# Turning the second layer's weights to float32 early, beside the first layer's steady blocks

## The chip, the cores and the metric

The kernel runs on one core of a Trainium2 chip. The metric is the device time of one execution in microseconds (us); of several runs the median counts. Five engines work side by side, each through its own instructions in order: PE multiplies matrices, DVE, ACT and POOL work on elements, and SP does nothing here but issue DMAs, that is, transfers between DRAM and the on-chip memory.

## The reference

Three stages follow each other. Between them the data stay in float32; the weight arrays `w_gate`, `w_val`, `w_out` of the first layer and `w_in`, `w_out` of the second come as float64.

```python
# attention in both directions, 8 batches of 8 heads; x: 512 rows, state: 32 rows
a  = softmax(scale * x @ state.T);   xread = a @ state
a2 = softmax(scale * state @ x.T);   sread = a2 @ x
x = concatenate([xread, sread])              # 8 * 544 = 4352 rows of 512
# first layer, d_ff = 1536
x = (silu(x @ w_gate) * (x @ w_val)) @ w_out
# second layer, d_ff = 2048
h = x @ w2_in
out = (h * sigmoid(1.702 * h)) @ w2_out      # 4352 x 512
```

## The kernel before

**Numbers in pieces.** Each float32 operand of a matmul is cut into a high part that TensorE takes whole and a low part that holds the rest, and a product is three matmuls: high by high, high by low, low by high. So a piece of weights ends as a tile `wu` with two halves. The loader of the weights is one ordered list, `stream`. Each entry is a unit of 128 by 512 weights (`("o", i, f)` for the first layer's output weights, `("i2", f)` and `("o2", f)` for the second layer's), with its source, its place, and a DRAM tile to keep it in, if any. Three functions walk along the list. `w_dma` issues loads into `raw`, of which there are four buffers; they are shared with `ev`, through which finished rows leave. `w_begin` does the conversion where the source is float64: two ACT operations (lines 192 and 193), two DVE operations (194 and 195) and an addition on POOL (198) make the float32 tile `wt`, of which there are three. Where the source is float32, `w_begin` issues nothing and only marks the raw buffer as held. `w_end` makes the halves: an ACT copy (208) and a POOL subtraction (209), and it stores the float32 tile where there is one to keep (211). `need(key)` brings the list forward to a unit: it ends units one after the other and keeps two more begun. Loads run at most four raw buffers ahead, held ones included, and two in the last two steps of a block (`pos["ahead"]`).

**First layer.** It runs in nine blocks, here called block 0 to 8 in order of time; blocks 0 to 6 and block 8 hold 512 rows of one batch, block 7 holds the 256 rows that belong to the states (`tail` in the code). A block has twelve steps `f`. A step makes a product for the gate and one for the value into two alternating `gv` buffers, applies the sigmoid (`sg`), multiplies, cuts the result into the halves of `h`, and adds the output product of the step before into `acc` (`out1`). In between, by the tables START, BLOCK0 and GROUP, stand the pieces of the attention of the next batch, and `state_weights`, which multiplies the states into the gate and value weights of the steps to come. These pieces put their products in `at`, of which there are two buffers, and PE takes such a buffer again only when ACT and DVE have emptied it. At the end of a block ACT and DVE copy `acc` into two `ev` tiles and SP stores them (`y`).

**Weights of the first layer.** Block 0 converts `w_out` once and keeps it in DRAM as float32 (`w1o`); blocks 1 to 8 load it from there, one unit per step.

**Weights of the second layer.** All 32 units are loaded as float64 and converted where they are used: four in block 7 (`NEW`), 24 in block 8, the last four in the first steps of the second layer. In the list an odd step of block 7 and each step of block 8 has its units behind the unit `("o", i, f)`.

The order on each engine is the order in which this Python code issues the instructions; no scheduler moves them.

Of the kernel before, what the change touches and what calls it, by code (L numbers as in the profile page):

```python
# [8 lines left out]
F32 = mybir.dt.float32  # L9
# [70 lines left out]
def kernel(  # L80
# [26 lines left out]
    DM = H * D  # L107
    FF1 = w_gate.shape[1]
    FF2 = w2_in.shape[1]
    P = 128  # L110
# [3 lines left out]
    F2 = FF2 // P  # L114
# [6 lines left out]
    v, a, pe, pool_e, sy = nc.vector, nc.scalar, nc.tensor, nc.gpsimd, nc.sync  # L121
# [6 lines left out]
    dp = ctx.enter_context(tc.tile_pool(name="scratch", bufs=1, space=DRAM))  # L128
# [12 lines left out]
    def f32(t):  # L141
        return t.bitcast(F32)


    def src_in(w, f):
        return w[:, f * P : (f + 1) * P].rearrange("(k p) m -> p k m", p=P)

    def src_out(w, f):
        return w[f * P : (f + 1) * P, :].unsqueeze(1)

    stream = []
# [5 lines left out]
    pos = {"dma": 0, "begun": 0, "done": 0, "ahead": 4}  # L157
    RAWS = 4

    def add(key, src, loc, keep=None):  # L160
        where[key] = len(stream)
        stream.append((key, src, loc, keep))
# [39 lines left out]
        pos["begun"] += 1  # L202

    def w_end():
        key, src, (pl, tag, bufs), keep = stream[pos["done"]]
        t = temps.pop(key)
        u = (pl or x2p).tile([P, 2, DM], F32R, name="wu", tag=tag, bufs=bufs)
        a.copy(u[:, 0, :], t)  # L208
        pool_e.tensor_tensor(u[:, 1, :], t, f32(u[:, 0, :]), op=ALU.subtract)  # L209
        if keep is not None:  # L210
            sy.dma_start(keep, t)
        held.discard(key)
        units[key] = u
        pos["done"] += 1

    def w_step(lead=2):
        if pos["begun"] > pos["done"]:
            w_end()
        w_dma()
        while pos["begun"] < min(pos["done"] + lead, len(stream)):  # L220
            w_begin()
            w_dma()
# [307 lines left out]
    def add_gv(u, k):  # L530
        r, c = slice(k * P, (k + 1) * P), slice(u * 2 * P, (u + 1) * 2 * P)
        add(("gv", u, k), (w_gate[r, c], w_val[r, c]), (wp, f"w{u * KD + k}", 1))
# [3 lines left out]
    for f in range(F1):  # L536
        if f < F1 - 2:
            for k in range(2):
                add_gv(f // 2 + 1, f % 2 * 2 + k)
        add(("o", 0, f), src_out(w_out, f), (wp, "o", 2), w1o[f])  # L540
    for i in range(1, NB1 - 2):
        for f in range(F1):
            add(("o", i, f), w1o[f], (wp, "o", 2))

    units2 = []
    for f in range(F2):
        units2.append((("i2", f), src_in(w2_in, f)))
        units2.append((("o2", f), src_out(w2_out, f)))
    NEW = 4
    x2p = None  # L550

# [34 lines left out]
    def h_tile(n):  # L586
# [14 lines left out]
        "attn_state": lambda: attn_state(0),  # L601
        "begin": w_begin,
        "end": w_end,
        "sw0": lambda: state_weights(0, 0, 0),
        "sw1": lambda: state_weights(0, 0, 1),
# [39 lines left out]
    for i, blk in enumerate(order1):  # L645
# [39 lines left out]
        def w_beside(ops):  # L685

            for op in ops if i == 0 else "":
                if op == "E":
                    if pos["begun"] > pos["done"] and pos["done"] < where["o", 1, 0]:
                        w_end()  # L690
                    continue
                w_dma()
                if pos["begun"] < min(pos["done"] + 2, len(stream)) and stream[pos["begun"]][0] in raws:
                    w_begin()
                    w_dma()
# [148 lines left out]
```

## Time and profile before

| | us |
|---|---|
| median of three runs | 1674.04 (1673.78 to 1674.15) |
| the profiled execution, its own time | 1674.44 |
| its span, first to last instruction | 1672.7 |
| block 0, with the start | about 200 |
| blocks 1 to 5, each | 90.2 |
| block 6 | 91.4 |
| block 7 (256 rows) | 61.0 |
| block 8 | 108.5 |
| second layer | about 760 |

PE is busy for 1568 us, 94% of the span, DVE for 51%, ACT for 41%, POOL for 21%. The shares differ by stage. In the profile's picture of 40 slices PE stands at nine tenths or more from the fifth slice on, except for slices 19 to 22, which are blocks 7 and 8; there POOL goes up from two tenths to as much as eight and DVE up to eight. The granted clock of TensorE is at one of two levels, 1.2 or 2.4 GHz; a row gives its mean over a stretch as a share of the higher one. A block's end is read from its `y` stores on SP. The time of one execution is the span and 1.7 us around it.

### The profile page before, as it was taken

The numbers are of one execution on the slowest core, as the hardware profiler recorded it, in microseconds if no ns is written. First come the engines' busy times: TensorE is split into PE (matmuls) and PEld (weight loads), VectorE is DVE, ScalarE is ACT, GpSimd is POOL, SyncE is SP. The second block draws the span as 40 slices with busy tenths as digits, with TensorE's granted clock in tenths as the row PEclk, the third lists the DMA queues.
The fourth block names the chain that finished last, engine by engine and source line by source line (L and its number), as shares of the span: only waits on it lengthen the run. The fifth ranks groups of instructions, "written<-read, shape, count | busy, mean of one in ns | idle before, by whom it ended". The sixth has DMA issues, their size and how long they took to land.

```text
span 1672.7 us, 18772 instructions
## 1 busy us (share of the span) xinstructions
PE 1568.0 (94%) x7100; PEld 1274.6 (76%) x7100; DVE 859.8 (51%) x1361; ACT 682.1 (41%) x1217; POOL 350.7 (21%) x263
## 2 busy tenths in 40 slices
PE   4667899999999999989987999999999999999997
PEld 2445688888888888869765888888888888888886
DVE  5788766676767666654787333232322322222222
ACT  5566554545555454544565232222222222222222
POOL 3566322222222221225686020000000000000000
PEclk7788899999999999999999999999999999999999
DMA  4445321212122212223445001010101010000000
GB/s 144 126 137 151 103 52 48 77 42 82 49 67 59 64 45 80 52 76 108 145 157 176 19 0 45 7 45 7 41 10 38 13 38 13 32 20 29 10 26 14
DMA packets 85747, 102.40 MB, mean 61 GB/s; under 512 B 44184, under 2 KB 53400, under 8 KB 85656
## 3 DMA queue, kind: packets, MB, share of 16 engines
q1 hardware_dynamic: 85656, 101.21, 20.1%
q8 instruction: 55, 0.90, 0.2%
q14 instruction: 36, 0.29, 0.1%
HBM read 79.69 MB, written 21.50 MB: 60 GB/s over the span
## 4 chain that ended last, share of the span: by engine, by line
PE 45%; DVE 4%; ACT 1%; issue 1%; DMA 0%; DVEq 0%
PE gv L236 8%; PE gv L235 8%; PE gv L234 8%; PE acc L247 7%; PE acc L246 7%; PE acc L248 7%; DVE wt L195 2%; DVE wt L194 1%; ACT wu L208 0%; ACT wt L192 0%; ACT h L736 0%; DVE sg L730 0%; DVE sg L720 0%; DVE xl L571 0%; DMA raw<-in_moe_w_in_dram 0%
## 5 line engine op out<-in xcount | busy, mean ns | idle before, releaser
L805 DVE TENSOR_TENSOR sg<-gv,sg 128x512 f32<-128x512 f32 (+1 forms) x144 | 95.3, 662 | 426.1 <-ACT sg L804 426.1
L804 ACT ACTIVATE sg<-gv 128x512 f32<-128x512 f32 (+1 forms) x144 | 82.6, 574 | 442.1 <-PE gv L236 442.1
L236 PE MATMUL gv<-xl,wu 128*128 128x512 f32 (+1 forms) x576 | 219.5, 381 | 0.0
L235 PE MATMUL gv<-xh,wu 128*128 128x512 f32 (+1 forms) x576 | 219.2, 381 | 0.0
L234 PE MATMUL gv<-xh,wu 128*128 128x512 f32 (+1 forms) x576 | 219.0, 380 | 0.0
L209 POOL TENSOR_TENSOR wu<-raw,wu 128x512 fp32r<-128x512 f32 x96 | 126.0, 1312 | 425.3 <-ACT wu L208 392.9
L247 PE MATMUL acc<-wu,h 128*128 128x512 f32 x544 | 213.2, 392 | 0.0
L246 PE MATMUL acc<-wu,h 128*128 128x512 f32 x544 | 212.9, 391 | 0.0
L248 PE MATMUL acc<-wu,h 128*128 128x512 f32 x544 | 212.1, 390 | 0.0
L241 PE MATMUL gv<-a,xh 128*128 128x512 f32 x384 | 160.6, 418 | 14.9 <-DVE sg L730 10.0
L242 PE MATMUL gv<-a,xl 128*128 128x512 f32 x384 | 157.6, 410 | 16.8 <-DVE xl L571 16.8
L679 PE MATMUL acc<-h,wu 128*128 128x512 f32 (+1 forms) x432 | 167.0, 387 | 4.8 <-ACT h L736 4.8
L680 PE MATMUL acc<-h,wu 128*128 128x512 f32 (+1 forms) x432 | 165.5, 383 | 0.9 <-POOL wu L209 0.9
L681 PE MATMUL acc<-h,wu 128*128 128x512 f32 (+1 forms) x432 | 165.2, 382 | 1.0 <-DVE h L738 0.9
L243 PE MATMUL gv<-a,xh 128*128 128x512 f32 x384 | 156.3, 407 | 0.0
L571 DVE TENSOR_TENSOR h<-sg,h 128x512 fp32r<-128x512 f32 (+1 forms) x144 | 96.4, 670 | 95.4 <-ACT h L570 90.0
L570 ACT CAST h<-sg 128x512 fp32r<-128x512 f32 (+1 forms) x144 | 86.0, 597 | 105.6 <-DVE sg L805 105.6
L234 PEld LDWEIGHTS gv<-xh,wu 128*128 128x128 f32 x576 | 108.5, 188 | 22.3
L235 PEld LDWEIGHTS gv<-xh,wu 128*128 128x128 f32 x576 | 108.2, 188 | 22.2
L236 PEld LDWEIGHTS gv<-xl,wu 128*128 128x128 f32 x576 | 108.3, 188 | 21.8
L720 DVE TENSOR_TENSOR sg<-gv,sg 128x512 f32<-128x512 f32 (+1 forms) x108 | 71.2, 659 | 95.5 <-ACT sg L718 95.1
L246 PEld LDWEIGHTS acc<-wu,h 128*128 128x128 f32 x544 | 102.1, 188 | 22.5
(105 smaller groups left out, 2728.0 us busy)
## 6 DMA issues: line engine op xcount, KB each, us to landing
raw<-w1o SPq DMA_DIRECT2D x96, 256.0 KB
raw<-in_moe_w_out_dram SPq DMA_DIRECT2D x28, 512.0 KB
y<-ev SPq DMA_DIRECT2D x16, 512.0 KB
raw<-in_moe_w_in_dram SPq DMA_DIRECT2D x16, 512.0 KB
xr<-y SPq DMA_DIRECT2D x32, 256.0 KB
out_dram<-ev SPq DMA_DIRECT2D x16, 512.0 KB
xn<-in_x_dram SPq DMA_DIRECT2D x14, 512.0 KB
raw<-in_moe_w_gate_dram SPq DMA_DIRECT2D x24, 256.0 KB
```

Of the source, the lines that this page charges most:

```text
L234: pe.matmul(ps[:, :N], wh, xh, start=k == 0, stop=False)
L235: pe.matmul(ps[:, :N], wl, xh, start=False, stop=False)
L236: pe.matmul(ps[:, :N], wh, xl, start=False, stop=k == KD - 1)
L241: pe.matmul(ps, wh, xh, start=k == 0, stop=False)
L242: pe.matmul(ps, wl, xh, start=False, stop=False)
L243: pe.matmul(ps, wh, xl, start=False, stop=k == len(pairs) - 1)
L246: pe.matmul(ps, lh, rh, start=first, stop=False)
L247: pe.matmul(ps, lh, rl, start=False, stop=False)
L248: pe.matmul(ps, ll, rh, start=False, stop=last)
L679: pe.matmul(ps, w[:, 0, c], h[:, 0, :N], start=f == 0, stop=False)
L680: pe.matmul(ps, w[:, 1, c], h[:, 0, :N], start=False, stop=False)
L681: pe.matmul(ps, w[:, 0, c], h[:, 1, :N], start=False, stop=f == F1 - 1)
```

## The change

32 new entries go into the list: a second layer's unit stands behind each odd step's `("o", i, f)` of blocks 1 to 5 and behind those of steps 1 and 3 in block 6. Such an entry has a place of `None`. It is loaded as float64 and converted by `w_begin` like any other; `w_end` then only stores its `wt` in a DRAM tile of float32 (`w2i`, `w2o`). The entries of blocks 7 and 8 and of the second layer have these DRAM tiles as their source, so that they are loaded as float32 and `w_begin` issues nothing for them. All 32 units are moved; nothing else is computed differently.

```diff
     def w_end():
-        key, src, (pl, tag, bufs), keep = stream[pos["done"]]
+        key, src, loc, keep = stream[pos["done"]]
         t = temps.pop(key)
+        if loc is None:
+            sy.dma_start(keep, t)
+            pos["done"] += 1
+            return
+        pl, tag, bufs = loc
         u = (pl or x2p).tile([P, 2, DM], F32R, name="wu", tag=tag, bufs=bufs)
...
+    sources = []
+    for f in range(F2):
+        sources.append((("i2", f), src_in(w2_in, f)))
+        sources.append((("o2", f), src_out(w2_out, f)))
+    units2 = [(key, dp.tile([P, DM], F32, name=f"w2{key[0]}{key[1]}")) for key, _ in sources]
+    turns = iter(zip(sources, units2))
     for i in range(1, NB1 - 2):
         for f in range(F1):
             add(("o", i, f), w1o[f], (wp, "o", 2))
-
-    units2 = []
-    for f in range(F2):
-        units2.append((("i2", f), src_in(w2_in, f)))
-        units2.append((("o2", f), src_out(w2_out, f)))
+            turn = next(turns, None) if f % 2 else None
+            if turn:
+                add(("turn", turn[0][0]), turn[0][1], None, turn[1][1])
```

Lines behind the first edit stand 5 higher in the changed kernel, lines behind the second 10 higher: line 208 is 213, 331 is 336, 571 is 581, 730 is 740.

SP at the end of block 2 and the start of block 3, before: two stores of `y`, then loads of the first layer's output weights.

```order
L759 DMA y_2_0_3082<-ev 128x1024
L759 DMA y_2_2_3087<-ev 128x1024
L174 DMA raw<-w1o_103 128x512
L174 DMA raw<-w1o_104 128x512
L174 DMA raw<-w1o_105 128x512
```

The same place now (line 208 is the new store):

```order
L769 DMA y_2_0_3221<-ev 128x1024
L769 DMA y_2_2_3226<-ev 128x1024
L208 DMA w2o_124<-wt 128x512
L177 DMA raw<-in_moe_w_in_dram 128x4x128
L174 DMA raw<-w1o_103 128x512
L174 DMA raw<-w1o_104 128x512
L177 DMA raw<-in_moe_w_out_dram 128x512
```

A store and a float64 load have moved in ahead of the first float32 load, and behind the stores of `y`; the float64 load waits until the first of these two stores has been read out, since it takes its buffer.

DVE in the first step of block 3, before (`stz`: the states; `xtl`: low part of the turned input of the attention; `xl`: low part from `state_weights`):

```order
L720 TENSOR_TENSOR sg<-gv,sg 128x512
L294 TENSOR_TENSOR stz_95<-at,stz_95 128x4x64
L730 TENSOR_TENSOR sg<-gv,sg 128x512
L335 TENSOR_TENSOR xtl_3134<-at,xth_3133 128x512
L571 TENSOR_TENSOR xl<-at,xh 128x512
L738 TENSOR_TENSOR h<-sg,h 128x512
```

And now:

```order
L730 TENSOR_TENSOR sg<-gv,sg 128x512
L299 TENSOR_TENSOR stz_95<-at,stz_95 128x4x64
L194 TENSOR_SCALAR wt<-wt 128x512
L195 SCALAR_TENSOR_TENSOR wt<-raw,wt 128x512
L740 TENSOR_TENSOR sg<-gv,sg 128x512
L340 TENSOR_TENSOR xtl_3282<-at,xth_3281 128x512
L581 TENSOR_TENSOR xl<-at,xh 128x512
L748 TENSOR_TENSOR h<-sg,h 128x512
```

The conversion of the unit behind step 1 stands in step 0, ahead of the work that empties `gv` and both `at` buffers. ACT has its two operations in the same place, ahead of the high part of the turned input:

```order
L298 CAST stz_95<-at 128x2x2x64
L300 COPY stz_95<-stz_95 128x2x2x64
L213 CAST wu<-raw 128x512
L192 ACTIVATE wt<-raw 128x512
L193 ACTIVATE raw<-raw 128x512
L336 CAST xth_3281<-at 128x512
L580 CAST xh<-at 128x512
L746 CAST h<-sg 128x512
```

DVE in step 8 of a steady block, before (`sq`, `sp`: sums and shares of the softmax; `ec`: turned shares):

```order
L720 TENSOR_TENSOR sg<-gv,sg 128x512
L730 TENSOR_TENSOR sg<-gv,sg 128x512
L400 TENSOR_REDUCE sq<-sp 128x16
L401 TENSOR_SCALAR sq<-sq 128x16
L402 RECIPROCAL sq<-sq 128x16
L405 TENSOR_TENSOR sp<-sp,sq 128x512
L571 TENSOR_TENSOR xl<-at,xh 128x512
```

And now:

```order
L730 TENSOR_TENSOR sg<-gv,sg 128x512
L194 TENSOR_SCALAR wt<-wt 128x512
L195 SCALAR_TENSOR_TENSOR wt<-raw,wt 128x512
L740 TENSOR_TENSOR sg<-gv,sg 128x512
L405 TENSOR_REDUCE sq<-sp 128x16
L406 TENSOR_SCALAR sq<-sq 128x16
L407 RECIPROCAL sq<-sq 128x16
L410 TENSOR_TENSOR sp<-sp,sq 128x512
L581 TENSOR_TENSOR xl<-at,xh 128x512
```

Here the conversion stands ahead of the softmax sums and of `xl`, whose `at` buffer the next `state_weights` on PE takes. Its ACT operations stand behind the two exponentials of this step.

## Rows read from the trace of the kernel before

**Rows 1.** Engines in a steady block, block 7, block 8: us, busy PE PEld DVE ACT POOL, clock, DMA.

```profile
290.60:380.90 90.30, 90.30 (x414) 73.88 (x413) 61.11 (x105) 45.60 (x81) 21.51 (x16) 1.00 0.22 61
743.00:804.00 61.00, 55.04 (x433) 54.09 (x432) 26.40 (x50) 25.01 (x54) 27.21 (x21) 0.94 0.38 117
804.00:912.50 108.50, 89.48 (x351) 66.91 (x350) 89.23 (x102) 68.14 (x126) 82.94 (x60) 0.95 0.54 167
```

**Rows 2.** Timeline of PE (start, duration): twelve matmuls in a row; block 8's first; layer two's first.

```profile
349.34 0.40 PE L241 MATMUL gv<-a,xh 128*128 128x512 f32 x1
...
351.92 0.39 PE L243 MATMUL gv<-a,xh 128*128 128x512 f32 x1
...
803.85 0.39 PE L241 MATMUL gv<-a,xh 128*128 128x512 f32 x1
...
912.11 0.39 PE L234 MATMUL gv<-xh,wu 128*128 128x512 f32 x1
```

**Rows 3.** Groups of instructions in block 8: count, busy us, mean ns of one, idle before.

```profile
L195 DVE SCALAR_TENSOR_TENSOR wt<-raw,wt 128x512 uint32<-128x512 uint32 x25 | 38.6, 1545 | 0.9
...
L194 DVE TENSOR_SCALAR wt<-wt 128x512 uint32<-128x512 uint32 x25 | 18.2, 729 | 11.4 <-ACT wt L192 11.4
```

**Rows 4.** Timelines of SP, ACT, DVE and PE at the start of block 7.

```profile
745.26 0.39 SPq L177 DMA_DIRECT2D raw<-in_moe_w_in_dram  x1
...
749.42 0.66 ACT L192 ACTIVATE wt<-raw 128x512 f32<-128x512 f32 x1 [5.60 <-DMA raw<-in_moe_w_in_dram]
...
750.11 0.43 DVE L194 TENSOR_SCALAR wt<-wt 128x512 uint32<-128x512 uint32 x1 [6.26 <-ACT wt L192]
...
750.57 0.69 DVE L195 SCALAR_TENSOR_TENSOR wt<-raw,wt 128x512 uint32<-128x512 uint32 x1
...
751.18 0.42 DVE L730 TENSOR_TENSOR sg<-gv,sg 128x256 f32<-128x256 f32 x1
...
751.65 0.58 PE L241 MATMUL gv<-xh,wu 128*128 128x256 f32 x1 [5.89 <-DVE sg L730]
```

**Rows 5.** Timelines of SP, ACT, DVE and PE at the start of block 3.

```profile
383.56 0.32 SPq L174 DMA_DIRECT2D raw<-w1o  x1
...
384.82 0.61 ACT L208 CAST wu<-raw 128x512 fp32r<-128x512 f32 x1
...
387.12 0.69 DVE L571 TENSOR_TENSOR xl<-at,xh 128x512 fp32r<-128x512 f32 x1 [0.47 <-ACT xh L570]
...
388.17 0.39 PE L241 MATMUL at<-wu,stz 128*128 128x512 f32 x1
```

**Rows 6.** Timelines of ACT and SP at the end of block 0.

```profile
200.34 0.59 ACT L582 COPY ev<-acc 128x512 f32<-128x512 f32 x1 [0.87 <-PE acc L681]
...
203.07 9.07 SPq L174 DMA_DIRECT2D raw<-w1o  x4
```

**Rows 7.** Timelines of ACT, POOL, DVE and PE around step 8 of block 2.

```profile
354.17 0.60 ACT L208 CAST wu<-raw 128x512 fp32r<-128x512 f32 x1
...
354.85 1.29 POOL L209 TENSOR_TENSOR wu<-raw,wu 128x512 fp32r<-128x512 f32 x1 [2.69 <-ACT wu L208]
...
354.29 0.69 DVE L400 TENSOR_REDUCE sq<-sp 128x16 f32<-128x512 f32 x1 [1.16 <-ACT sp L392]
...
355.01 1.16 DVE L401 TENSOR_SCALAR sq<-sq 128x16 f32<-128x16 f32 x1
...
357.10 0.68 DVE L571 TENSOR_TENSOR xl<-at,xh 128x512 fp32r<-128x512 f32 x1
...
358.10 0.39 PE L241 MATMUL at<-wu,stz 128*128 128x512 f32 x1
```

**Rows 8.** Timeline of PE in block 8: two matmuls behind short waits.

```profile
818.55 0.50 PE L241 MATMUL gv<-a,xh 128*128 128x512 f32 x1 [1.76 <-DVE sg L730]
...
853.48 0.50 PE L241 MATMUL gv<-a,xh 128*128 128x512 f32 x1 [1.74 <-DVE sg L730]
```

**Rows 9.** Engines in a short stretch behind the first of these waits; columns as in rows 1.

```profile
819.80:823.10 3.30, 3.30 (x9) 2.59 (x8) 2.36 (x4) 3.30 (x7) 2.76 (x2) 0.51 0.51 187
```

## The prediction, made blind

> **What bounds the kernel now.** I read the picture of 40 slices first, then the table of engines by stage, then the time lines around the places where the stage changes. In the steady blocks PE is busy without a break, 90.3 of 90.3 us at the full clock, while ACT works half of the time, DVE two thirds and POOL a quarter [rows 1]. There only what makes PE wait can cost anything. Blocks 7 and 8 are different. Block 8 has 351 matmuls where a steady block has 414, and still takes 108.5 us; POOL is busy for 83 of them and DVE for 89 [rows 1]. So it is bound by the turning of weights: DVE spends 57 us there on lines 194 and 195 alone, and line 195 takes 1.55 us on average, where it takes 0.69 with POOL at rest [rows 3, 4]. In block 7 one thing stands out: the first float64 load is issued at 745.26, ACT waits for it in its queue until 749.42, DVE waits for ACT, and with DVE the emptying of a gv buffer, so that PE stands still for 5.9 us [rows 4]. The second layer has PE busy from end to end and keeps its instructions, apart from its last four units.
>
> **What is taken away.** Block 8 loses the five conversion operations of 24 units. What is left on POOL is 36 subtractions of about 1.3 us, 47 us, and on DVE 89 - 57 = 32 us; neither is near the time of the matmuls, so PE becomes the bound. Twelve matmuls in a row start 2.58 us apart from first to last, 0.2345 us each [rows 2]. Block 8 has 288 for its two products and 60 for the states' weights, so it needs 348 x 0.2345 = 81.6 us. From its first matmul to the first of the second layer it takes 912.11 - 803.85 = 108.3 us [rows 2]. The gain is 26.7 us. In block 7 the wait of 5.9 us goes, since a float32 unit issues nothing in `w_begin`; what is late next is the ACT copy of that unit a step later, behind work enough for a load of half the size. With the wait goes slow time: a granted clock of 0.94 over 61 us is 7.3 us at half speed, of which the wait covers at most 5.9, so that between 0.7 and 3.6 us of matmul time were lost; I take 1.3, since most of the wait's end lies in the slow stretch. Together 7.2 us from block 7 and **33.9 us of gain**.
>
> **What is added, in general.** Each of the 32 moved units costs ACT two operations (1.3 us), DVE two (1.1 us alone, up to 2.3 beside POOL), POOL one (1.3), SP a load of 512 KB and a store of 256 KB, all inside blocks 1 to 6. That is some 8 us per engine and block, against free time of 45 us on ACT, 29 on DVE and 69 on POOL [rows 1]: by shares it is hidden. But each engine takes its instructions in order, so I went through the six places in a block where a conversion now stands (steps 0, 2, 4, 6, 8 and 10) and asked what PE needs next from behind it. At steps 2, 4, 6 and 10 I find between half a microsecond and two of room and put the cost at nothing; if that room is gone, each of these some 20 places costs up to 1 us.
>
> **Step 0, blocks 2 to 6.** Loads run only two ahead at a block's end, so the unit behind step 1 is loaded late: after the stores of `y`, when the first has given up its buffer. In the trace that point is 383.56 for block 3, where a float32 load starts now [rows 5]. The conversion's ACT operations come right behind the copy at 384.82 [rows 5] and wait for the landing. The only float64 load of the trace that stands so, at the start of block 7, took 749.42 - 745.26 = 4.16 us [rows 4]; so ACT starts at 383.56 + 4.16 = 387.7. From there to the start of line 730 on DVE are 751.18 - 749.42 = 1.76 us [rows 4]; then come 730, the low part of the turned input and `xl`, three operations with 0.6, 0.6 and 0.7 us. At 387.72 + 1.76 + 1.9 = 391.4 the `at` buffer is free for which PE's `state_weights` wait; PE wanted it at 388.17, when DVE had long begun on it [rows 5]. The stall is 3.2 us, five times 16.2. Bounds: with a landing after 2.7 us, as the 512 KB store at the end of block 0 has it (the second copy at 200.34, the load behind it at 203.07 [rows 6]), it is 1.8 us; with 1.3 us more for the new store ahead in the queue, 4.5.
>
> The Trainium skill, "DMA: Bandwidth & Descriptors", section "Anatomy of one DMA", puts a transfer at 2.0 us and its bytes over 436 GB/s, for another path of issue than this one; for 512 KB an estimate by it is 3.2 us, and the five stalls would cost 4.8 us less together. The row has 4.16 us, so I leave the sum at that.
>
> **Step 0, block 1.** Here the unit is loaded early, in block 0, and so takes a third raw buffer; the second pair of `ev` copies then waits until the first store of `y` has landed, at 203.07, not 200.34 [rows 6]. ACT has 1.5 us of slack behind it, so 1.2 us of the shift of 2.7 remain, and the two conversion operations add 1.2 to 2 on ACT and DVE; less 0.4 us of room before PE asks, 2.0 to 2.8. I take 2.5.
>
> **Step 8, blocks 1 to 5.** ACT's conversion stands behind the copy at 354.17, so from 354.7 [rows 7]. POOL is subtracting from 354.85 to 356.14; line 194 can hardly end before that, as line 401 next to it shows, which takes 1.16 us and ends with POOL [rows 7]. So 194 and 195 end at 357.1, line 730, which had been done at 353, at 357.7; the sums that began at 354.29 follow [rows 7], and the chain up to `xl` takes another 1.9 to 2.5 us, with POOL's addition of the new unit in the way of line 401 again. `xl` ends at about 360.2; PE asks for its buffer at 358.10 [rows 7]. The stall is 2.1 us, five times 10.5; without POOL in the way it would be 1.5, with both collisions in full 2.8.
>
> **The clock.** These eleven stalls stand in a stretch that has run at 2.4 GHz throughout. The trace shows stalls with and without a fall: after the wait of 5.9 us in block 7 the clock was half, after one of 1.76 us in block 8 it was half for 3.3 us [rows 4, 8, 9], after one of 1.74 it was not [rows 8]. Such a fall costs half of 3.3, 1.7 us. Mine are of 3.2 and 2.1 us; I count four falls among the six longer ones and two among the five shorter, 6 x 1.7 = 10.2 us. The bounds are 0 and 18.7.
>
> **Sum.** 16.2 + 2.5 + 10.5 + 10.2 = 39.4 us against 33.9: 5.5 us longer. The profiled execution took 1674.4 us (span 1672.7), so 1679.9; the median of the runs lies 0.4 below it: **1679.5 us**, slower by 0.3%.
>
> **Rivals.**
> *The stalls come, the clock stays up.* For it: the waits of about 1.7 us that had no fall, and that my stalls are each followed by many microseconds of unbroken matmuls. Against it: the fall after 1.76 us. Then 29.2 against 33.9: 1674.0 - 4.7 = 1669.3, faster. It decides as soon as fewer than about three stalls are followed by a fall. Chance 0.25.
> *The steady blocks take it all in.* For it: the shares of rows 1. The landing would have to come within a microsecond of its issue and step 8 to have 2 us of room that I don't see. All of the gain would stay: 1674.0 - 33.9 = 1640.1, or some 1655 if step 8 alone costs nothing and the clock stays. Chance 0.08.
> *Block 8 doesn't come down to its matmuls.* A float32 unit holds its raw buffer from its load to the end of POOL's subtraction, and four buffers must pass 36 units, nine each; in 81.6 us one may take 9.1 us. Load, copy and subtraction in a row are 4.2 + 0.6 + 1.3 = 6.1 us, so it needs 3 us of waiting in the queues besides. If a cycle is 10 us, block 8 takes 90 us, and the time is 1679.5 + 8.4 = 1688. Chance 0.12.
> That the change doesn't move what it says is out: the order has no 192 to 198 behind block 6.
>
> **Chances.** The forecast has 0.55, and with it a spread from 1672 (two falls) to 1688 (all stalls at their upper bounds). 0.2%, about what a measurement of this kernel can tell from no change, is 3.3 us, so the limits are 1670.7 and 1677.4. Slower: 0.44 of the forecast and 0.10 of the last rival. Same: 0.11 of the forecast, 0.10 of the first rival and 0.02 of the last. Faster: 0.15 and 0.08. The range: 1662, which leaves out most of the second rival, to 1690.
>
> **What would show it.** Block 8 in some 81 us with PE busy throughout, and block 7 without its wait (the gain); at the start of blocks 2 to 6 an ACT line 192 that waits for the load of `w_in`, and PE waiting some 3 us on DVE; in step 8 of blocks 1 to 5 some 2 us on DVE's `xl`; blocks 1 to 5 at 95 to 99 us each in place of 90.2; granted clock below 1.00 in them. The prediction is wrong if these blocks stay at 90 to 92 us, or block 8 over 90.

## The result, and the profile after

The changed kernel took **1687.2 us** (median of four runs, 1686.1 to 1687.9) where the kernel before took 1674.1: a ratio of 1.0077, 95% interval 1.0060 to 1.0095. It is slower, by 13.1 us where 5.5 were forecast. The profiled execution took 1687.5 us, its span 1685.7.

First the stages. The view is that of rows 1: a stretch, its length, the busy time of PE, PEld, DVE, ACT and POOL, the granted clock, DMA share and GB/s. The first two stretches are two steady blocks from one store of `y` to the next, the others block 7 and block 8.

```profile
298.00:397.00 99.00, 93.96 (x414) 75.90 (x413) 66.95 (x117) 52.62 (x93) 29.32 (x22) 0.97 0.36 103
397.00:496.10 99.10, 93.99 (x414) 75.94 (x413) 66.95 (x117) 52.62 (x93) 29.25 (x22) 0.97 0.35 103
...
787.00:843.00 56.00, 56.00 (x448) 54.86 (x446) 18.77 (x43) 20.57 (x46) 20.71 (x16) 1.00 0.31 95
843.00:924.80 81.80, 81.73 (x359) 66.46 (x358) 36.47 (x54) 42.10 (x78) 48.18 (x36) 1.00 0.47 136
```

Beside rows 1: a steady block went from 90.3 to 99 us with the same 414 matmuls, and PE, which had been busy throughout, has 5 us of idle time and a clock of 0.97. In the stretches shown, block 8 went from 108.5 to 81.8 us, block 7 lost its idle time, and both run at full clock. From one store of `y` to the next, block 7 is 7.6 us shorter (53.3 after 60.9) and block 8 is 28.4 shorter (80.2 after 108.6): 36.0 us of gain. The five blocks 1 to 5 took 97.0, 99.0, 99.1, 99.8 and 99.0 us in place of 90.2, and block 6 took 96.3 in place of 91.4. With 0.7 us in block 0 and 0.8 in layer two, that is 49.1 us of cost.

Next, what PE waited for between 200 and 960 us (total, count, longest).

```profile
PE at L347 <- DVE xtl L340: 18.0, 6, 4.0
PE at L246 <- DVE xl L581: 10.1, 5, 2.0
PE at L246 <- DVE stz L299: 0.7, 1, 0.7
```

The first line is step 0 of blocks 1 to 6, the second step 8 of blocks 1 to 5, the third the start of block 1. The timeline of SP, ACT, DVE and PE at step 0 of block 2 (start, duration, and in brackets the idle time ahead with what ended it) answers to rows 4 and 5:

```profile
299.81 0.38 SPq L208 DMA_DIRECT2D w2o<-wt  x1
...
300.72 0.38 SPq L177 DMA_DIRECT2D raw<-in_moe_w_in_dram  x1
...
301.96 0.61 ACT L213 CAST wu<-raw 128x512 fp32r<-128x512 f32 x1
...
304.92 0.66 ACT L192 ACTIVATE wt<-raw 128x512 f32<-128x512 f32 x1 [2.35 <-DMA raw<-in_moe_w_in_dram]
...
305.61 0.43 DVE L194 TENSOR_SCALAR wt<-wt 128x512 uint32<-128x512 uint32 x1 [3.99 <-ACT wt L192]
...
306.07 0.69 DVE L195 SCALAR_TENSOR_TENSOR wt<-raw,wt 128x512 uint32<-128x512 uint32 x1
...
307.28 0.68 DVE L340 TENSOR_TENSOR xtl<-at,xth 128x512 fp32r<-128x512 f32 x1
...
308.02 0.50 PE L347 MATMUL at<-xth,stz 128*128 128x512 f32 x1 [3.01 <-DVE xtl L340]
```

The float64 load is issued at 300.72, behind the store of the unit before it. ACT stands for it from 302.6 to 304.9, DVE stands for ACT, and everything that DVE still owes to this step, `xtl` among it, comes behind. PE's next product in its order (L347, the scores) needs the `at` buffer that `xtl` empties, so PE stands for 3.01 us. In step 8 of the same block it is the order on ACT and DVE, with no load in it (beside rows 7):

```profile
365.95 0.61 ACT L397 ACTIVATE sp<-sp 128x512 f32<-128x512 f32 x1
...
366.98 0.66 ACT L192 ACTIVATE wt<-raw 128x512 f32<-128x512 f32 x1
...
367.15 1.29 POOL L214 TENSOR_TENSOR wu<-raw,wu 128x512 fp32r<-128x512 f32 x1 [2.69 <-ACT wu L213]
...
367.73 1.00 DVE L194 TENSOR_SCALAR wt<-wt 128x512 uint32<-128x512 uint32 x1 [3.09 <-ACT wt L192]
368.77 0.69 DVE L195 SCALAR_TENSOR_TENSOR wt<-raw,wt 128x512 uint32<-128x512 uint32 x1
...
371.86 0.68 DVE L581 TENSOR_TENSOR xl<-at,xh 128x512 fp32r<-128x512 f32 x1
...
372.60 0.50 PE L246 MATMUL at<-wu,stz 128*128 128x512 f32 x1 [2.02 <-DVE xl L581]
```

DVE idles for 3.09 us until ACT has come to L192 behind the exponentials, and then has L194, L195 and its own sums ahead of `xl`. L194 takes 1.00 us here and 0.43 in step 0: here POOL is at L214 as it starts, in step 0 POOL is free.

Last, the clock. Ten short stretches of blocks 1 to 6 ran at half speed, one behind each wait of two microseconds or more (a fall of the clock, from here on). Here are four of them, and the stretch between the first two; the windows begin 0.3 us late, so that their mean is 0.54 and not 0.50:

```profile
275.25:278.66 3.41, 3.41 (x13) 2.83 (x12) 3.09 (x6) 1.10 (x2) 1.69 (x1) 0.54 0.78 169
309.38:312.79 3.41, 3.41 (x10) 2.71 (x9) 1.66 (x3) 1.10 (x2) 0.37 (x1) 0.54 0.42 145
374.23:377.64 3.41, 3.41 (x13) 2.82 (x12) 3.08 (x6) 1.10 (x2) 1.66 (x1) 0.54 0.75 169
408.37:411.78 3.41, 3.41 (x10) 2.68 (x9) 1.75 (x3) 1.18 (x3) 0.20 (x1) 0.54 0.38 145
278.66:308.00 29.34, 26.34 (x120) 21.20 (x119) 14.80 (x30) 12.64 (x25) 6.30 (x5) 1.00 0.34 109
```

The first and third follow the wait of step 8, the second and fourth that of step 0. Half of 3.4 us is 1.7 us lost each time, as an estimate, while PE shows as busy. The two short waits at the start of block 1 (0.72 and 1.49 us) had no such stretch behind them.

### The profile page after: what moved, and what is told of

It is laid out like the page before. It is cut to its first block, busy times and chain, and to the rows that moved or that the text cites. A ratio compares the mean times of both kernels' runs of the same rounds, so it can differ in the third digit from the quotient of the medians.

```text
span 1685.7 us, 18930 instructions
## 1 busy us (share of the span) xinstructions
PE 1583.0 (94%) x7100; PEld 1287.5 (76%) x7100; DVE 825.7 (49%) x1361; ACT 685.4 (41%) x1217; POOL 345.1 (20%) x263
## 5 line engine op out<-in xcount | busy, mean ns | idle before, releaser
L214 POOL TENSOR_TENSOR wu<-raw,wu 128x512 fp32r<-128x512 f32 x128 | 168.4, 1321 | 501.2 <-ACT wu L213 426.3
L814 ACT ACTIVATE sg<-gv 128x512 f32<-128x512 f32 (+1 forms) x144 | 82.9, 576 | 448.2 <-PE gv L241 448.2
L247 PE MATMUL gv<-a,xl 128*128 128x512 f32 x384 | 160.8, 419 | 16.2 <-DVE xl L581 16.2
L246 PE MATMUL gv<-a,xh 128*128 128x512 f32 x384 | 162.3, 423 | 0.7 <-ACT xh L580 0.7
L248 PE MATMUL gv<-a,xh 128*128 128x512 f32 x384 | 159.4, 415 | 0.0
L728 ACT ACTIVATE sg<-gv 128x512 f32<-128x512 f32 (+1 forms) x108 | 62.1, 575 | 141.5 <-PE gv L248 141.2
```

The lines of the kernel that those rows point to most:

```text
L246: pe.matmul(ps, wh, xh, start=k == 0, stop=False)
L247: pe.matmul(ps, wl, xh, start=False, stop=False)
L248: pe.matmul(ps, wh, xl, start=False, stop=k == len(pairs) - 1)
```

## The experiments

All kernels are variations of the changed one. In most of them one line is edited, the one that says behind which of the first layer's units a float64 unit stands in the stream. Which step then converts it is read from the trace, since the line alone does not settle it: three of the expectations below name a step that the kernel did not use, and this is said at each. Waits and falls are counted in one profiled execution of each kernel.

### Gain and cost apart

```diff
-    units2 = [(key, dp.tile([P, DM], F32, name=f"w2{key[0]}{key[1]}")) for key, _ in sources]
+    units2 = [(key, w1o[n % F1]) for n, (key, _) in enumerate(sources)]
...
-            turn = next(turns, None) if f % 2 else None
+            turn = None
```

> The gain alone: blocks 1 to 6 as in the kernel before (nothing of layer two is loaded, turned or stored there), blocks 7 and 8 load float32 units as in after. The units that they load are the first layer's float32 weights, since nobody has turned the second layer's: layer two computes with other weights, the work and its time are the same. Theory: blocks 7 and 8 gain what after shows there (7.6 + 28.4 = 36.0 us) and nothing else changes: 1674.1 - 36.0 = 1638. Rival (part of what blocks 1 to 6 lose in after is not their extra work but a delay that is owed to the blocks' end, and part of blocks 7 and 8's gain is owed to the earlier blocks): between 1638 and 1650, with blocks 7 and 8 longer than 53.3 and 80.2 us.

Measured: 1639.0 us (1638.3 to 1639.6), 1638 expected. The steady block, block 7 and block 8 of this kernel, columns as above:

```profile
200.63:290.84 90.21, 90.21 (x414) 73.81 (x413) 61.09 (x105) 45.55 (x81) 21.55 (x16) 1.00 0.23 61
...
743.17:796.46 53.29, 53.22 (x433) 52.48 (x432) 17.46 (x40) 19.41 (x44) 20.71 (x16) 1.00 0.33 100
796.46:876.67 80.21, 80.21 (x348) 65.08 (x348) 35.88 (x52) 41.57 (x77) 48.18 (x36) 1.00 0.46 138
```

Blocks 7 and 8 have the lengths that they have in the changed kernel, and PE is at its matmuls throughout. The counterpart has the cost alone:

```diff
             if turn:
                 add(("turn", turn[0][0]), turn[0][1], None, turn[1][1])
+    units2 = sources
```

> The cost alone: blocks 1 to 6 turn and store the second layer's weights as in after, blocks 7 and 8 load them as float64 and turn them again, as in the kernel before; the stored float32 copies are not read. Theory: gain and cost add, so this is before plus the 49 us that after's blocks 0 to 6 and layer two lost: 1674.1 + 49 = 1723, and with the kernel that has the gain alone, the two differences sum to that of after (+13.0). Rival (the waits of blocks 2 to 6 come and go with where a block stands, as the kernel with three units loaded ahead shows of the clock's falls): 1700 to 1715, if the falls are fewer.

Measured: 1721.3 us (1720.8 to 1723.9), 1723 expected. The ten long waits in blocks 1 to 6 stand where the changed kernel has them, with nine falls behind them. Against the 1673.9 us of the kernel before in the same runs, gain alone is -34.9 and cost alone +47.4; their sum, +12.5, is the change's own +13.1 within the measurements' spread. So the two halves do not touch each other, and the rest is a question about blocks 1 to 6 only. There the changed kernel lost 47.6 us. The 0.8 us of layer two belong to the gain's side: from block 8's store of `y` to the end the kernel with the gain alone takes 760.9 us, the kernel before and the one with the cost alone 760.1.

### Away from step 0, away from step 8

```diff
-            turn = next(turns, None) if f % 2 else None
+            turn = next(turns, None) if f in (3, 5, 7, 8, 9, 11) else None
```

> The kernel after, but the float64 unit that blocks 1 to 6 turn in step 0 is turned in step 7 instead; the other five units of a block stay in steps 2, 4, 6, 8 and 10. Theory (the place decides: in step 0 the unit's late load of 4.2 us and its operations hold up xtl and xl, TensorE waits 3.0 to 4.0 us in blocks 2 to 6 and 0.72 + 1.49 us in block 1, and each of the five long waits is followed by 3.4 us at half the clock, so 1.7 us more): the waits at L347 in step 0 go, the falls drop from 10 to 5, and the time falls by 16.5 + 2.2 + 8.5 = 27 us to about 1660. Rival 1 (the price is that of an extra 512 KB load, an extra store and six extra operations in a block wherever they stand): the total stays at 1685 to 1689, with waits of 2 to 4 us in step 7. Rival 2 (the falls of the clock are not caused by the step's wait): the waits go and the falls stay, about 1668.

Measured: 1649.6 us (1648.5 to 1650.0), 10 below the theory and far from both rivals. The waits of step 0 are gone, but more went with them. The trace shows the unit that was to be in step 7 in step 8, ahead of L213, and the one behind it pushed on into step 9, where it costs nothing: the conversions stand in steps 2, 4, 6, 8, 9 and 10. Waits of PE between 200 and 960 us, then the timeline of step 8 of block 2:

```profile
PE at L246 <- DVE xl L581: 8.3, 5, 1.7
```

```profile
356.27 0.64 ACT L192 ACTIVATE wt<-raw 128x512 f32<-128x512 f32 x1
...
357.00 0.43 DVE L194 TENSOR_SCALAR wt<-wt 128x512 uint32<-128x512 uint32 x1 [2.56 <-ACT wt L192]
...
359.55 1.28 POOL L214 TENSOR_TENSOR wu<-raw,wu 128x512 fp32r<-128x512 f32 x1
...
359.95 1.43 DVE L410 TENSOR_TENSOR sp<-sp,sq 128x512 f32<-128x512 f32 x1
...
362.03 0.50 PE L246 MATMUL at<-wu,stz 128*128 128x512 f32 x1 [1.66 <-DVE xl L581]
```

ACT comes to L192 one cast earlier, so the wait is 1.66 us and not 2.02, though L410 now meets POOL and takes 1.43 us in place of 0.69. And no wait of this kernel is followed by a fall of the clock. The theory had left five waits of 2.0 us and five falls, 18.5 us; what stayed is 8.3 us and none, 10.2 less, which is the miss.

L410 reads two tensors in SBUF, and ends 0.55 us after POOL's subtraction. The Trainium skill, "SBUF — State Buffer", section "Who interferes with whom", says that such a VectorE instruction contends with a GpSimd instruction that reads SBUF. This pair of rows agrees: 1.43 us beside POOL, 0.69 without it.

```diff
-            turn = next(turns, None) if f % 2 else None
+            turn = next(turns, None) if f in (1, 3, 5, 7, 10, 11) else None
```

> The kernel after, but the unit that blocks 1 to 6 turn in step 8 is turned in step 9 instead; the others stay in steps 0, 2, 4, 6 and 10. Theory (step 8 is the one other bad place, since there ScalarE's exponentials stand ahead of the unit's conversions and DVE's work on them stands ahead of xl): the 2.0 us waits at L246 in step 8 of blocks 1 to 5 go, the falls drop from 10 to 5, the time falls by 5 x (2.0 + 1.7) = 18.5 us to about 1668.7. Rival (extra operations cost the same in any step): about 1687, with waits of 1 to 2 us in step 9.

Measured: 1676.2 us (1674.9 to 1678.2), 7.5 more than the theory. Steps: 0, 2, 4, 6, 9 and 11. The wait of step 8 is gone, step 9 costs nothing here either, but the last unit has slid into step 11, and five new waits of 1.2 us stand at the ends of blocks 1 to 5, 6.0 us in all. The five waits of step 0 are as they were, with four falls. The timeline of ACT, POOL and PE at the end of block 3 shows the reason:

```profile
481.97 0.67 ACT L192 ACTIVATE wt<-raw 128x512 f32<-128x512 f32 x1
...
483.10 0.61 ACT L213 CAST wu<-raw 128x512 fp32r<-128x512 f32 x1
...
484.01 1.31 POOL L198 TENSOR_TENSOR wt<-wt,raw 128x512 uint32<-128x512 uint32 x1 [7.51 <-DVE wt L195]
...
485.27 1.72 POOL L214 TENSOR_TENSOR wu<-raw,wu 128x512 fp32r<-128x512 f32 x1
...
487.05 0.50 PE L690 MATMUL acc<-h,wu 128*128 128x512 f32 x1 [1.21 <-POOL wu L214]
```

POOL must add up the float64 unit (L198) before it may split the first layer's last unit (L214), which PE needs for the block's last product.

```diff
-            turn = next(turns, None) if f % 2 else None
+            turn = next(turns, None) if f in (3, 5, 7, 8, 10, 11) else None
```

> Both moves at once: the six units of a block are turned in steps 2, 4, 6, 7, 9 and 10. Theory: no wait of over 1 us and no fall of the clock in blocks 1 to 6, the time is that after less 27 and less 18.5, about 1642, that is 32 us below the kernel before: the gain of blocks 7 and 8 (36.0 us) is kept and some 4 us are paid (blocks 1 to 5 at about 90.5 to 91 us each). Rival (the moved units find new waits in steps 7 and 9, at 1 to 2 us each in six blocks): 1655 to 1670.

Measured: 1656.7 us (1655.9 to 1657.8), in the rival's range. Steps: 2, 4, 6, 8, 9 and 11, so it avoided step 0 alone. Its waits are those of the two kernels above, five of 1.67 us in step 8 and five of 1.2 us in step 11, with no fall; a steady block takes 93.7 us.

### What in step 0 and in step 8 costs the time

```diff
-            pos["ahead"] = 4 if f < F1 - 2 else 2
+            pos["ahead"] = 4 if f < F1 - 2 else 3 if 0 < i < 6 else 2
```

> The kernel after, with the units in their places, but three units instead of two are loaded ahead of the end of blocks 1 to 5, so that the float64 unit of step 0 lies in SBUF before that step asks for it. Theory A (the late load decides: ACT stands 2.35 us for it): TensorE's wait in step 0 of blocks 2 to 6 shrinks from 3.0 to 4.0 us to what block 1 shows with its load early, 0.7 + 1.5 us at most in two parts, and their five falls of the clock go: 5 x (3.3 + 1.7) = 25 less 5 x 0 to 2.2, so 1662 to 1674. Theory B (the unit's operations on ScalarE, VectorE and GpSimd decide, whenever it was loaded): the waits stay at 2.5 us and over, the falls too, 1682 to 1688. Also possible: the third buffer held by the unit delays the output's evictions of the block's end, which share the four buffers; then a new wait appears there at the end of the block, and the total does not fall.

Measured: 1671.3 us (1670.1 to 1675.7), theory A. The units are where they were; only the load of step 0's is early. Its wait of 3.0 to 4.0 us became two, as in block 1 (0.69 and 1.53 us), but for block 4, which has one of 2.13. That is 11.0 us in blocks 2 to 6 where it was 16.5. The wait of step 8 is as it was, five times 2.0 us, 10.1 in all. Yet the clock fell twice, not ten times: once behind a wait of step 8, once behind that of 2.13. The falls were the larger part of what this kernel won back. What is left in step 0 has a cause of its own (what was waited for between 200 and 960 us):

```profile
ACT ev L592 <- DMA y<-ev: 22.8, 6, 5.0
...
PE at L347 <- DVE xtl L340: 7.6, 5, 1.5
...
PE at L246 <- DVE stz L299: 5.6, 6, 2.1
```

The early unit holds one more of the four raw buffers, so at the end of each of blocks 0 to 5 ACT's second copy of finished rows waits for the first store of `y`, and `stz` comes late behind it. The edit thus trades the late load for a late buffer; how much of the 2.2 us left in a block is owed to the buffer and how much to the conversions, it does not show.

```diff
+            if f == 8 and i > 0:
+                need(("o", i, f))
             run(f, 0)
```

> The kernel after, with the unit of step 8 at the same step and loaded at the same time, but its two conversions on ScalarE (L192, L193) and the cast before them (L213) stand ahead of the two exponentials of the state instead of behind them; all else is as in after, step 0 too. Theory (the order decides: behind the exponentials, VectorE's L194 waits 3.09 us for L192 and then takes 1.7 us with L195, and L740, L405 to L410 and xl all stand behind it): moved ahead, the pair runs on VectorE while it would idle, and xl comes some 1.4 us earlier, since the exponentials themselves end 1.7 us later; TensorE's wait in step 8 falls from 2.02 to about 0.6 us, and no fall of the clock follows it: 1687 - 5 x (1.4 + 1.7) = about 1672. Rival (the unit's operations on VectorE and GpSimd are too much for step 8 wherever they stand in it): the wait stays at 1.6 to 2.0 us, 1679 to 1687.

Measured: 1670.8 us (1668.5 to 1672.1), 1672 expected. ACT, DVE and PE in step 8 of block 2:

```profile
360.55 0.67 ACT L192 ACTIVATE wt<-raw 128x512 f32<-128x512 f32 x1
...
361.30 1.00 DVE L194 TENSOR_SCALAR wt<-wt 128x512 uint32<-128x512 uint32 x1 [0.44 <-ACT wt L192]
...
363.81 0.62 ACT L397 ACTIVATE sp<-sp 128x512 f32<-128x512 f32 x1
...
364.46 0.69 DVE L405 TENSOR_REDUCE sq<-sp 128x16 f32<-128x512 f32 x1 [0.83 <-ACT sp L397]
...
367.03 0.50 PE L246 MATMUL at<-wu,stz 128*128 128x512 f32 x1 [0.23 <-DVE xl L581]
```

The same five operations in the same step, L194 again 1.00 us beside POOL, and PE's wait is 0.23 us. The three casts and conversions ahead of the exponentials use the time in which DVE had idled for 3.09 us. So step 8 is a matter of order, on ACT and with it on DVE and POOL. The five falls behind it are gone; those behind the waits of 3.05 to 4.18 us in step 0, which this kernel keeps, came five times out of five.

### A place for all six

```diff
-            turn = next(turns, None) if f % 2 else None
+            turn = next(turns, None) if f in (3, 4, 5, 6, 7, 11) else None
```

> The six float64 units of a block stand behind the units 3, 4, 5, 6, 7 and 11 of the first layer; the order on ScalarE puts their conversions into steps 2, 4, 5, 6, 7 and 10 of a block, so that none is in step 0, 8 or 11, the three steps that showed waits (3.0 to 4.0 us, 1.7 to 2.0 us and 1.2 us). Theory (the place alone decides, and steps without the state's exponentials and without a block's boundary have room on ScalarE, VectorE and GpSimd): no wait over 0.5 us and no fall of the clock in blocks 1 to 6, each block within 0.7 us of the 90.2 us of before, the total at 1638 to 1643. Rival (a unit in a step next to another unit's finds ScalarE and GpSimd still at the one before, and holds up the first layer's own unit, as step 11 showed with L690 waiting 1.2 us for L214): one or two new waits of 1.2 to 1.7 us in each block, 1647 to 1660.

Measured: **1639.2 us** (1638.9 to 1639.7), a ratio of 0.9793 to the kernel before, 95% interval 0.9778 to 0.9807. Two steady blocks, and all that PE waited for between 200 and 960 us:

```profile
200.43:290.66 90.23, 90.23 (x414) 73.79 (x413) 68.45 (x117) 52.33 (x93) 30.11 (x22) 1.00 0.39 111
290.66:380.89 90.23, 90.23 (x414) 73.81 (x413) 68.44 (x117) 52.32 (x93) 30.08 (x22) 1.00 0.39 114
```

```profile
PE at L635 <- DMA tt<-sread: 0.4, 1, 0.4
```

The block has the same 117 DVE, 93 ACT and 22 POOL instructions as the changed kernel's, with as much traffic, and takes 90.2 us as before the change. The kernel that turns no weights in these blocks took 1639.0. So the work costs nothing that can be measured, and the 47.6 us that blocks 1 to 6 lost came from where it stood.

### The wait of step 8 by itself, and the clock

```diff
-            turn = next(turns, None) if f % 2 else None
+            turn = next(turns, None) if f in (3, 4, 5, 7, 9, 11) else None
```

> Units behind the first layer's units 3, 4, 5, 7, 9 and 11: the conversions stand in steps 2, 4, 5, 6, 8 and 10. It is the kernel whose six units cost nothing (steps 2, 4, 5, 6, 7 and 10, 1639.2 us) with the unit of step 7 put back into step 8, behind the exponentials, where it stood in after; step 0 has none. The wait of 2.0 us at L246 in step 8 comes back in blocks 1 to 5, that is 10.1 us. The question is the clock. Theory A (a wait of 2.0 us is followed by a fall of its own, as after showed in five blocks of five): 5 x 1.7 us more, 1639.2 + 10.1 + 8.5 = 1657.8. Theory B (the wait's length alone does not decide: in the kernel with three units loaded ahead, the same wait of 2.0 us was followed by a fall in one or two blocks of five): 0 to 2 falls, 1649.3 to 1652.7.

Measured: 1653.6 us (1653.3 to 1654.8), 0.9 above theory B and 4 below theory A. The first two and the fourth of blocks 1 to 5, from store to store, and then the 6.7 us behind the wait of step 8 in the second and the fourth of them:

```profile
199.65:293.75 94.10, 92.07 (x414) 74.94 (x413) 66.66 (x117) 52.55 (x93) 29.80 (x22) 0.98 0.37 106
293.75:387.80 94.05, 92.03 (x414) 74.97 (x413) 66.32 (x117) 52.52 (x93) 30.28 (x22) 0.98 0.38 109
...
480.32:572.87 92.55, 90.52 (x414) 73.76 (x413) 66.43 (x117) 52.56 (x93) 30.31 (x22) 1.00 0.39 111
```

```profile
363.39:370.00 6.61, 6.61 (x26) 5.56 (x27) 5.71 (x12) 2.75 (x6) 1.81 (x1) 0.74 0.70 189
...
549.97:556.70 6.73, 6.73 (x33) 5.69 (x34) 5.91 (x13) 2.75 (x6) 1.82 (x1) 1.00 0.73 191
```

The same wait of 2.02 us in five blocks; behind the first two of them the clock fell, behind the other three it did not: 26 matmuls were begun in the one stretch and 33 in the other. A block with a fall is 1.5 us longer. Without one the block is 92.53 - 90.22 = 2.3 us longer than an undisturbed one, so each wait costs 0.3 us beyond its own length. Two kernels above agree: 92.17 us with one wait of 1.66, and 93.68 with waits of 1.67 and 1.20. Why it is so was not looked into.

## Why the prediction was right, and which term was off

**Blocks 7 and 8: right.** 33.9 us of gain were forecast and 36.0 came, 26.7 and 7.2 against 28.4 and 7.6. Block 8 is bound by its matmuls: from its first matmul to that of layer two are 80.6 us, the sum had 81.6. The rival that four buffers hold it up to 90 us did not happen. Its time, 1688, is what was measured, but by coincidence: the blocks that it has slow were fast, and the time was lost in blocks 1 to 5. In block 7 the clock was half for 3.3 us behind the old wait (751.7 to 755.0), 1.7 us lost where the sum had 1.3: 5.9 + 1.7 is the 7.6 that came.

**Step 0 and step 8: right in place and size, and in mechanism but for one operand.** The waits were to be 5 x 3.2, 2.5 and 5 x 2.1, together 29.2 us. They are 16.5 us in blocks 2 to 6, 0.72 + 1.49 in block 1 and 10.1 in step 8, together 28.8. The landing that was taken from block 7's row, 4.16 us, came as 304.92 - 300.72 = 4.20, and in blocks 2 to 6 as 3.8 to 4.5; the 1.3 us for the new store ahead in the queue, a bound for which the prediction has no row, did not show. The estimate of 3.2 us by the Trainium skill, "DMA: Bandwidth & Descriptors", section "Anatomy of one DMA", which speaks of another path of issue, is not borne out on this one. The operand was another than forecast: PE was to stand at `state_weights` until `xl` had emptied its buffer, and it stood one product earlier, at the scores, until `xtl` had. Both the need (387.71 in place of 388.17 in the kernel before) and the release came about half a microsecond sooner, so the length came out right all the same. In step 8 the second meeting of line 401 (now L406) with POOL did not take place: it ended in 0.24 us. The ordering kernel confirms the cause in step 8: with the unit ahead of the exponentials the wait is 0.2 us. The loading kernel confirms that of step 0 in part: with the load early its waits fall by a third, from 16.5 to 11.0 us, and with no unit there they go. Steps 2, 4, 6 and 10 were put at nothing, and are nothing.

**The clock: mis-sized, and it is the miss.** Six falls of 1.7 us were counted, ten came, one behind each wait of two microseconds or more. At 1.5 to 1.7 us each that is 15 to 17 us where the sum had 10.2: 5 to 7 us of the 7.6 between 5.5 and 13.1. The count was interpolated from two waits of 1.75 us, one with a fall and one without; for the long ones that was too low. The trace of before held better rows: beside the wait of 5.9 us one more long one, at the end of block 8, and the clock was half behind it too:

```profile
906.89 0.79 PE L679 MATMUL acc<-h,wu 128*128 128x512 f32 x1 [4.82 <-ACT h L736]
```

```profile
906.90:911.90 5.00, 5.00 (x12) 3.82 (x13) 4.53 (x6) 3.87 (x7) 3.52 (x4) 0.50 0.69 204
```

Of its four waits of 1.73 to 1.76 us only the first had a fall. A smaller term was left out: each wait costs 0.3 us beyond its length, some 3.5 us for twelve. It is offset in part by 2.1 us more of gain. Of the other 1.5 us, 0.8 are layer two's (above, cause open), and the 0.7 of block 0 lie within what that block varies by, 199.6 to 201.4 us over the eleven traces.

**What was luck.** Ten falls at 1.5 us are some 15 us, more than the whole difference of 13.1. With two falls, as in the kernel with the early load, the same waits would by this estimate have given about 1675, next to no change, and with none about 1672. So that it came out slower hung on the count that the prediction had least ground for.

**The rivals.** That the clock stays up was given 0.25 and 1669 us. It did not happen in this kernel. The one with step 0's load early, with two falls, took 1671, but its waits are 5.5 us shorter too. That the steady blocks take it all in was given 0.08 and 1640 us: with the units in these places it is wrong; with other places it is what happens, at 1639.2. Its side remark, 1655 if step 8 alone costs nothing and the clock stays, does not follow from the prediction's own terms, by which it is 1640.1 + 16.2 + 2.5 = 1658.8. The weighing of shares against order in the prediction was thus sound: the shares told truly that there is room, and the order told truly that there is none at these two places, as the operations stood there.

**What stays open.** What decides whether a wait is followed by a fall. Waits of 3.0 to 4.2 us in step 0 had one in five of five blocks (the changed kernel, that with the cost alone, and that with step 8's unit moved ahead) and in four of five (the kernel with steps 9 and 11). Waits of 2.0 us in step 8 had one in five of five (the changed kernel), four of five (cost alone), two of five (step 8 alone) and one of five (early load). Waits of 1.67 us (two kernels) and of 1.2 us had none. So length matters but does not settle it alone. Why all ten came in the changed kernel is not shown; the kernel with the cost alone has the same order in blocks 1 to 6 and had nine.

## What to carry to other kernels

Work that fits into the free shares of the engines can be moved beside a saturated TensorE for nothing, if at each place one asks whether a load, or an engine that is busy just then, stands between it and the next operand that TensorE needs: the same units, six in a block, cost 47 us in one order and nothing beyond the spread of the runs in another. Do not put an instruction that waits for a late load into the queue of an engine that feeds TensorE at the start of a block, and put side work ahead of a long operation whose result the next engine waits for, not behind it. Read where a moved step lands from the trace or the order, not from the line that moves it, and count on a possible fall of the clock behind a stall of TensorE of two microseconds or more.

## What the runs showed of the hardware

- A wait of 2 us can cost nearly as much again: in the kernel with step 8 alone the same wait of 2.02 us cost 2.3 us without a fall and 3.9 us with one (blocks of 92.5 and 94.1 us against 90.2), and PE shows as busy in all of the slow stretch.
- Equal waits in equal blocks of one execution need not agree in that: two of five fell.
- The lengthening of VectorE's instructions beside GpSimd hit other lines whenever the order moved: L194 took 1.00 us in step 8 and 0.43 with POOL at rest; L410 1.43 and 0.69. By itself it did not make TensorE wait: in steps 6 and 10 of block 2 of the changed kernel L194 took 0.99 and 1.00 us too, and no wait followed.
